# Moving the output stores and token loads of a two-layer MoE kernel's second part from SyncE's queue to GpSimd's

## The chip, the cores and the metric

The kernel runs on one core of a Trainium2 chip. The metric is the device time of one execution in microseconds. Before the change the median of three runs is 1465.66 us (1464.34 to 1467.58).

## The reference

The reference computes attention with pooled keys and values, then two feed-forward layers, all in float32:

```python
k_p = k.reshape(B, H, Sp, pool, D).mean(axis=3)        # B = H = 8, S = 576, D = 64, pool = 8
v_p = v.reshape(B, H, Sp, pool, D).mean(axis=3)
attn = softmax(q @ k_p^T / sqrt(D))                    # (its sum gets 1e-9 added)
x = (attn @ v_p) as 4608 tokens x 512
h = maximum(maximum(x @ w1, x @ w2), x @ w3)           # d_ff 768
x = h @ moe_w_out                                      # 4608 x 512
h = maximum(x @ w_in, 0.0)                             # d_ff 2048
out = (h * h) @ w_out                                  # 4608 x 512
```

## The kernel before

Each operand of the large products is split into a high and a low part (`split`: ScalarE rounds the high part, VectorE or GpSimd subtracts it), and a product is three matmuls: high by high, high by low, low by high.

**Part 1**, to 753 us, is attention and the first layer, in 12 blocks of 384 tokens. Its results, the tokens of the second layer, are written to `y_dram`. Beside it, the second layer's weights are combined, split and written to `wi_dram` and `wo_dram`. The change touches nothing of part 1.

**Part 2** is the second layer, in nine blocks (`NB2`, here called blocks 0 to 8) of 512 tokens. Each matrix product of 2 x 2 sub-matrices is done with seven products of sums and differences in place of eight. A block has four groups of hidden units (`gr` 0 to 3, here groups 0 to 3), each with two steps:

- `moe2_in` runs seven products of tokens `y` and weights `wi2s` (L688, 12 matmuls each), into PSUM tiles `ps` of which there are three. VectorE adds each to what came before (L659, tiles `c` and `a`); ScalarE and VectorE square.
- `moe2_out` runs four products in groups 0 and 1 and ten in groups 2 and 3 (L812, 12 matmuls each) into the PSUM tiles accA, accB, accD, accE and accF. Each has an operand `g`, made by `operand` and `split` (L134 on ScalarE, L135 on VectorE), and a weight tile `wo2s` of 512 KB, used once. In groups 2 and 3 the order is B, A, E, A, D, D, B, F, E, F.

The weights `wi2s` stay in SBUF. The tiles `wo2s` are fetched anew for every product (`fetch_out`, L616), 28 in a block, into a pool of five buffers (`wo_p`). So the fetch for a product can start when the fifth product before it has ended.

Block `j + 1`'s tokens are loaded by `load_y` (L631) while block `j` is in group 2. There are four tiles `yr`, each in two parts, and a part that spans two first-layer blocks takes two transfers, so a block has 8 or 12. The tiles share their places with operands of groups 0 to 2 and can be loaded when these have been read. `mix_y` and `split_y` then make seven operands `y` of the four tiles, on VectorE and ScalarE, beside group 3; the first of these is the difference `t<-yr` (L662). `evacuate` sums the accumulators and calls `store_out` (L768) four times in group 3: `o`, `o`, `qB`, `qA`, 256 KB each.

All these transfers are issued by SyncE, which issues in order, and waits for a transfer's buffer or data before it goes on to the next. The order on each engine is set by the tile scheduler, which simulates the program while it is built and places each instruction when its inputs and its engine are ready in that simulation. Moving a transfer to another queue so moves instructions on the other engines as well.

Of the kernel before, what the change touches and what calls it, by code (L numbers as in the profile page):

```python
# [20 lines left out]
P = 128  # L21
# [15 lines left out]
NB2 = NT // T2  # L37
# [57 lines left out]
def attention_moe_kernel(ctx: ExitStack, tc: tile.TileContext, q, k, v, vn, w1, w2, w3, wo1, wi2, wo2, out):  # L95
    nc = tc.nc
# [11 lines left out]
    for sign, base in ((1, POOL * MID), (-1, POOL - 1 - POOL * MID)):  # L108
        nc.gpsimd.affine_select(
            out=sums, in_=sums, compare_op=ALU.is_ge, fill=0.0, base=base,  # L110
# [8 lines left out]
    y_dram = [dram.tile([KD, P, T1], F32, name=f"y_dram{j}") for j in range(NB1)]  # L119
# [462 lines left out]
    for f in range(0, KF2, 2):  # L582
        rows = []
# [3 lines left out]
        rows = []  # L587
# [31 lines left out]
    def shared_place(i, shape, name):  # L619
        return y_p.tile(shape, F32, tag=f"r{i}", name=name)  # L620

    def load_y(j):

        for n, (r, h) in enumerate(((0, 0), (0, 1), (1, 0), (1, 1))):
            yr = shared_place(n, [P, 2, HT], "yr")
            for i in range(2):
                t = 0
                while t < HT:
                    b, o = divmod(j * T2 + h * HT + t, T1)
                    n = min(HT - t, T1 - o)  # L630
                    nc.sync.dma_start(out=yr[:, i, t : t + n], in_=y_dram[b][2 * r + i, :, o : o + n])  # L631
                    t += n
            yr_t[j, r, h] = yr

# [28 lines left out]

    ORDER = (1, 6, 7, 5, 2, 4, 3)
    early = [functools.partial(load_y, 0), functools.partial(mix_y, 0)]
    early.append(functools.partial(fetch_in, 0, w2_p))
    early += [functools.partial(split_y, 0, m) for m in ORDER]
# [97 lines left out]

    def store_out(j, half, d, o):
        rows = out[j * T2 + half * HT : j * T2 + (half + 1) * HT, d * 256 : (d + 1) * 256]
        nc.sync.dma_start(out=rows.rearrange("(i p) d -> p i d", p=P), in_=o.rearrange("p (i d) -> p i d", i=2))  # L768

    def evacuate(j, b, n):  # L770

        acc = made[b][0]
        if b in "AB" and n == HALF:
            q = made["q" + b] = c_p.tile([P, T2], F32, tag="q" + b, name="q" + b)
            nc.scalar.activation(q, acc, AF.Copy)
        if n < FULL[b]:
            return
        q = made["qA"]
        if b == "A":
            o = c_p.tile([P, T2], F32, tag="c3", name="o")  # L780
            nc.scalar.activation(o, acc, AF.Copy)
            store_out(j, 0, 0, o)
        elif b == "D":
            add(q, acc, q)
        elif b == "B":
            o = c_p.tile([P, T2], F32, tag="c2", name="o")
            add(o, acc, q)
            store_out(j, 1, 0, o)
        elif b == "E":
            add(q, acc, q)  # L790
            add(made["qB"], made["qB"], q)
            store_out(j, 1, 1, made["qB"])
        else:
            add(q, acc, q)
            store_out(j, 0, 1, q)
        del made[b]
# [32 lines left out]
    for j in range(NB2):  # L829
        for gr in range(NG):  # L830
            more = j + 1 < NB2
            c = moe2_in(j, gr)

            if gr == NG - 1 and more:
                mix_y(j + 1)
                for y in ORDER[:4]:
                    split_y(j + 1, y)
            for n, (m, h) in enumerate(OUT[gr >= NG // 2]):
                if gr == NG - 1 and more and n in (4, 6, 8):
                    split_y(j + 1, ORDER[2 + n // 2])  # L840
                moe2_out(j, gr, m, h, c)
            if gr == NG - 2 and more:
                load_y(j + 1)
            nxt = j * NG + gr + 1
            if nxt < NB2 * NG:
                fetch_group(nxt % NG)
# [41 lines left out]
```

## Time and profile before

| | |
|---|---|
| runs, median of 3 | 1465.66 us (1464.34 to 1467.58) |
| the profiled execution: its time | 1463.68 us |
| the profiled execution: its span, first to last instruction | 1462.0 us |
| part 2, from 753.3 us on | 708.7 us |
| TensorE / VectorE / ScalarE / GpSimd busy over the span | 98% / 67% / 52% / 12% |
| mean granted clock of TensorE, share of full speed | 0.993 |
| transfers by SyncE's queue | 261.61 MB |

A profile covers one execution. Engines are PE (TensorE's matmuls), PEld (its weight loads), DVE (VectorE), ACT (ScalarE), POOL (GpSimd) and SP (SyncE); "SPq" is SyncE's queue, whose time is not counted as busy. A row names the line of the kernel, the operation and its tiles as out<-in. In the timeline a row is a run of instructions of one group: its start and length in microseconds, how many, and in brackets the idle time before it and what ended it. Matmuls are pipelined, so their shown lengths overlap.

### The profile page before, as it was taken

To read this page: it belongs to the slowest core of one execution; us is meant where nothing else is said; L and a number is where in the kernel's file an instruction comes from. 1 tells how busy PE (TensorE), PEld (TensorE's weight loads), DVE (VectorE), ACT (ScalarE), POOL (GpSimd) and SP (SyncE) were. 2 spreads that over 40 slices of the span, in tenths; PEclk is the share of its full clock that TensorE was granted. 3 is DMA by queue.
4 is the path that set the end of the run, shared out by engine and by line. 5 is a ranking of instruction groups with operands and counts; after the bars stand their busy time and mean duration, and the time that the engine had idled before them with its cause. 6 is when DMAs were issued, how large, how long until landed. Compare 5 with 4: busy or idle time off the path is not lost.

```text
span 1462.0 us, 27667 instructions
## 1 busy us (share of the span) xinstructions
PE 1426.7 (98%) x10410; PEld 1401.6 (96%) x10410; DVE 983.3 (67%) x1778; ACT 762.5 (52%) x1983; POOL 177.5 (12%) x229
## 2 busy tenths in 40 slices
PE   6889999999999999999999999999999999999998
PEld 4879999999999999999999999999999999999998
DVE  5896476766765856756336768686766768686775
ACT  7795366664666656654323545363534445454443
POOL 3441022311312212221000000000000000000000
PEclk9999999999999999999999999999999999999999
DMA  7654145543455544432549857666567665665746
GB/s 226 188 164 140 62 145 181 173 137 130 145 170 187 151 145 144 127 123 86 187 162 356 280 176 240 220 208 217 214 231 230 229 212 213 205 238 179 277 139 229
DMA packets 125029, 272.81 MB, mean 187 GB/s; under 512 B 13504, under 2 KB 69568, under 8 KB 124896
## 3 DMA queue, kind: packets, MB, share of 16 engines
q1 hardware_dynamic: 117984, 261.61, 53.4%
q10 hardware_dynamic: 6912, 9.44, 1.8%
q8 instruction: 82, 1.34, 0.4%
q14 instruction: 51, 0.42, 0.1%
HBM read 213.91 MB, written 48.23 MB: 179 GB/s over the span
## 4 chain that ended last, share of the span: by engine, by line
PE 89%; DMA 6%; ACT 3%; DVE 2%; issue 1%; SPq 0%; POOL 0%; DVEq 0%; ACTq 0%; POOLq 0%
PE ps L528 29%; PE ps L688 23%; PE ps L547 10%; PE accB L812 6%; PE accA L812 6%; PE accF L812 3%; DMA wo2s<-wo_dram 3%; PE accE L812 3%; PE accD L812 2%; PE sc L362 2%; ACT ss L367 1%; PE tr L395 1%; PE av L425 1%; PE av L424 1%; DMA kq<-in_k_dram 1%
## 5 line engine op out<-in xcount | busy, mean ns | idle before, releaser
L528 PE MATMUL ps<-x,w 128*128 128x384 f32 x2592 | 493.8, 341 | 5.3 <-ACT w L134 2.7
L528 PEld LDWEIGHTS ps<-x,w 128*128 128x128 f32 x2592 | 449.6, 189 | 8.5 <-ACT w L134 3.0
L688 PE MATMUL ps<-y,wi2s 128*128 128x256 f32 x3024 | 371.5, 277 | 0.5 <-DVE c L659 0.2
L688 PEld LDWEIGHTS ps<-y,wi2s 128*128 128x128 f32 x3024 | 356.6, 188 | 1.5 <-DVE a L659 0.7
L547 PE MATMUL ps<-h,wo 128*128 128x384 f32 x864 | 162.2, 339 | 0.1
L547 PEld LDWEIGHTS ps<-h,wo 128*128 128x128 f32 x864 | 149.2, 188 | 0.7 <-POOL wo L135 0.4
L701 ACT ACTIVATE c<-c 128x512 f32<-128x512 f32 x90 | 56.3, 627 | 169.7 <-DVE c L659 169.1
L659 DVE TENSOR_TENSOR c<-ps,c 128x512 f32<-128x512 f32 x144 | 98.2, 687 | 67.3 <-PE ps L688 64.4
L536 DVE TENSOR_TENSOR hm<-ps,hm 128x384 f32<-128x384 f32 x144 | 79.6, 552 | 76.6 <-PE ps L528 73.6
L134 ACT ACTIVATE g<-c 128x512 fp32r<-128x512 f32 x144 | 90.3, 627 | 56.9 <-DVE c L698 23.3
L812 PE MATMUL accA<-wo2s,g 128*128 128x256 f32 x864 | 115.7, 277 | 0.0
L812 PE MATMUL accB<-wo2s,g 128*128 128x256 f32 x864 | 111.1, 277 | 4.5 <-DMA wo2s<-wo_dram 3.5
L812 PEld LDWEIGHTS accB<-wo2s,g 128*128 128x128 f32 x864 | 104.0, 188 | 5.7 <-issue 1.9
L135 DVE TENSOR_TENSOR g<-c,g 128x512 fp32r<-128x512 f32 x144 | 97.8, 685 | 16.5 <-ACT g L134 16.4
L812 PEld LDWEIGHTS accA<-wo2s,g 128*128 128x128 f32 x864 | 107.1, 188 | 0.0
L367 ACT ACTIVATE ss<-sc,st 128x72 f32<-128x72 f32 (+1 forms) x320 | 98.0, 321 | 15.0 <-DVE st L364 12.0
L373 POOL TENSOR_TENSOR ss<-ss,st 128x432 f32<-128x432 f32 (+1 forms) x64 | 53.7, 839 | 238.8 <-DVE st L372 96.4
L400 DVE TENSOR_TENSOR pt<-tr,pt 72x192 fp32r<-72x192 f32 (+1 forms) x112 | 48.8, 448 | 46.5 <-ACT pt L399 44.9
L427 ACT ACTIVATE xf<-av 64x192 f32<-64x192 f32 (+1 forms) x112 | 45.4, 405 | 58.8 <-PE av L425 47.5
L428 DVE TENSOR_TENSOR xf<-av,xf 64x192 f32<-64x192 f32 (+1 forms) x112 | 50.8, 453 | 36.7 <-ACT xf L427 34.8
L134 ACT ACTIVATE h<-hm 128x384 fp32r<-128x384 f32 x72 | 37.6, 522 | 57.1 <-DVE hm L536 56.4
L367 ACT ACTIVATION_READ_ACCUMULATOR ss<-sc,st 128x1 f32 (+1 forms) x320 | 66.3, 207 | 0.0
(107 smaller groups left out, 1936.5 us busy)
## 6 DMA issues: line engine op xcount, KB each, us to landing
wo2s<-wo_dram SPq DMA_DIRECT2D x252, 512.0 KB
wi2s<-wi_dram SPq DMA_DIRECT2D x24, 512.0 KB
wraw<-in_wo_dram SPq DMA_DIRECT2D x22, 512.0 KB
wraw<-in_w_dram SPq DMA_DIRECT2D x18, 512.0 KB
y_dram<-ys ACTq DMA_DIRECT2D x48, 192.0 KB
wraw<-in_wi_dram SPq DMA_DIRECT2D x16, 512.0 KB
wi_dram<-wraw SPq DMA_DIRECT2D x16, 512.0 KB
wo_dram<-wraw SPq DMA_DIRECT2D x64, 128.0 KB
```

Source lines behind the costliest of these rows:

```text
L134: nc.scalar.activation(hi, src, AF.Copy)
L135: engine.tensor_tensor(out=lo, in0=src, in1=as_f32(hi), op=ALU.subtract)
L367: nc.scalar.activation(ss[:, i, h], src[:, i, h], AF.Exp, bias=st[:, 0, i, h : h + 1], accum_out=st[:, 1, i, h : h + 1],)
L373: nc.gpsimd.tensor_tensor(out=ss, in0=ss, in1=st[:, 2].rearrange("p g (h o) -> p g h o", o=1).to_broadcast([m, g, 2, SP]), op=ALU.mult,)
L428: nc.vector.tensor_tensor(out=xf[r], in0=av[r], in1=xf[r], op=ALU.add)
L528: nc.tensor.matmul(ps, lhsT=w1_t[f, e][:, a, kk * P : (kk + 1) * P], rhs=x[kk][:, c], start=(n == 0), stop=(n == 3 * KD - 1),)
L536: nc.vector.tensor_tensor(out=hm, in0=ps, in1=hm, op=ALU.max)
L547: nc.tensor.matmul(ps, lhsT=wo1_t[kk][:, a, d * P : (d + 1) * P], rhs=hs[kk][:, c], start=(n == 0), stop=(n == 3 * KF1 - 1),)
L659: nc.vector.tensor_tensor(out=out, in0=in0, in1=in1, op=ALU.add)
L688: nc.tensor.matmul(bank[:, u * HT : (u + 1) * HT], lhsT=wi2_t[2 * gr + u][i][:, a, o + kk * P : o + (kk + 1) * P], rhs=y_t[j][m][:, c, kk] ...
L701: nc.scalar.activation(c, c, AF.Relu)
L812: nc.tensor.matmul(bank[:, i * 256 : (i + 1) * 256], lhsT=g[:, a, u * HT + i * P : u * HT + (i + 1) * P], rhs=w[:, u, c], start=(n == 0 an ...
```

## The change

The diff is whole:

```diff
     def load_y(j):
 
+        queue = nc.gpsimd if j else nc.sync
         for n, (r, h) in enumerate(((0, 0), (0, 1), (1, 0), (1, 1))):
             yr = shared_place(n, [P, 2, HT], "yr")
             for i in range(2):
@@
-                    nc.sync.dma_start(out=yr[:, i, t : t + n], in_=y_dram[b][2 * r + i, :, o : o + n])
+                    queue.dma_start(out=yr[:, i, t : t + n], in_=y_dram[b][2 * r + i, :, o : o + n])
@@
     def store_out(j, half, d, o):
         rows = out[j * T2 + half * HT : j * T2 + (half + 1) * HT, d * 256 : (d + 1) * 256]
-        nc.sync.dma_start(out=rows.rearrange("(i p) d -> p i d", p=P), in_=o.rearrange("p (i d) -> p i d", i=2))
+        queue = nc.gpsimd if j + 1 < NB2 else nc.sync
+        queue.dma_start(out=rows.rearrange("(i p) d -> p i d", p=P), in_=o.rearrange("p (i d) -> p i d", i=2))
```

The token loads of blocks 1 to 8 (84 transfers) and the stores of blocks 0 to 7 (32) are issued by GpSimd. Block 0's loads, in part 1, and the last block's stores stay with SyncE. Lines after L624 have one or two added to their numbers.

On SyncE, before, this stands where block 6's tokens are loaded in block 5 (`yr` are the token tiles, `wo2s` the weights, the numbers behind y_dram its blocks, counted from 128):

```order
L631 DMA yr<-y_dram_136 128x128
L631 DMA yr<-y_dram_137 128x128
L616 DMA wo2s<-wo_dram_0_0_116 128x1024
L631 DMA yr<-y_dram_136 128x256 x2
L616 DMA wo2s<-wo_dram_0_0_108 128x1024
```

On GpSimd, after, the same loads and the stores of the block stand like this, and SyncE has the weights alone:

```order
L632 DMA yr<-y_dram_136 128x128
L632 DMA yr<-y_dram_137 128x128
L632 DMA yr<-y_dram_136 128x256 x4
L770 DMA out_dram<-o 128x2x256 x2
L770 DMA out_dram<-qB 128x2x256
L770 DMA out_dram<-qA 128x2x256
```

The loads and stores have moved from between the weights to one queue of their own, the loads first.

On TensorE, before, in group 3 of block 5, from the last matmuls of the first accA product (the x4 of accA, which end it) to the second accB product:

```order
L812 MATMUL accA<-wo2s,g 128x256 x4
L812 MATMUL accE<-wo2s,g 128x256 x8
L812 MATMUL accA<-wo2s,g 128x256 x12
L812 MATMUL accD<-wo2s,g 128x256 x8
L688 MATMUL ps<-y_14434,wi2s_1_8638 128x256 x2
L812 MATMUL accD<-wo2s,g 128x256 x16
L812 MATMUL accB<-wo2s,g 128x256 x12
```

After, the same place, from the accA row whose first four matmuls end the first accA product (`ps<-y` belongs to the next block):

```order
L814 MATMUL accA<-wo2s,g 128x256 x12
L689 MATMUL ps<-y_14431,wi2s_2_8299 128x256
L689 MATMUL ps<-y_14434,wi2s_1_8297 128x256
L814 MATMUL accE<-wo2s,g 128x256 x4
L814 MATMUL accD<-wo2s,g 128x256 x8
L689 MATMUL ps<-y_14434,wi2s_1_8297 128x256 x5
L689 MATMUL ps<-y_14434,wi2s_1_8638 128x256 x3
L814 MATMUL accA<-wo2s,g 128x256 x4
L689 MATMUL ps<-y_14434,wi2s_1_8638 128x256 x3
L689 MATMUL ps<-y_14431,wi2s_2_8299 128x256
L814 MATMUL accB<-wo2s,g 128x256 x8
```

More of the next block's matmuls stand inside the group, and the second accB product, the seventh of the group, starts before the first accD product has ended. Between the end of the first accA product, which frees the seventh product's weight buffer, and the start of that product there were 46 matmuls and are 38.

On VectorE, before, in block 5, from the last operand of group 2 on (`t<-yr` is the first use of the next block's tokens, `c<-ps` the additions of group 3):

```order
L135 TENSOR_TENSOR g<-c_14013,g 128x512
L662 TENSOR_TENSOR t_14424<-yr 128x512
L659 TENSOR_TENSOR c_14316<-ps,c_14315 128x512
L135 TENSOR_TENSOR y_14427<-yr,y_14427 128x512
L662 TENSOR_TENSOR yr<-yr 128x512
L659 TENSOR_TENSOR yr<-yr 128x512
L659 TENSOR_TENSOR c_14317<-ps,c_14316 128x512
```

After:

```order
L135 TENSOR_TENSOR g<-c_14013,g 128x512
L660 TENSOR_TENSOR c_14316<-ps,c_14315 128x512
L660 TENSOR_TENSOR c_14317<-ps,c_14316 128x512
L660 TENSOR_TENSOR c_14318<-ps,c_14317 128x512
L660 TENSOR_TENSOR c_14315<-ps,c_14315 128x512
L663 TENSOR_TENSOR t_14424<-yr 128x512
L135 TENSOR_TENSOR y_14504<-yr,y_14504 128x512
```

The first use of the tokens has moved from before the first addition to behind the fourth. In blocks 1, 2, 4, 5 and 7, where the next block's tokens come in twelve transfers, it stands behind four or five additions (before, behind one or none); in blocks 3 and 6 behind one and in block 0 behind four, as it did.

## Rows read from the trace of the kernel before

**Rows 1.** The page: busy time of the engines, and the chain that ended last.
```profile
PE 1426.7 (98%) x10410; PEld 1401.6 (96%) x10410; DVE 983.3 (67%) x1778; ACT 762.5 (52%) x1983; POOL 177.5 (12%) x229
...
PE 89%; DMA 6%; ACT 3%; DVE 2%; issue 1%; SPq 0%; POOL 0%; DVEq 0%; ACTq 0%; POOLq 0%
```

**Rows 2.** Busy time by stretch: block 0, blocks 1 to 7, the rest.
```profile
core 0: us, PE busy (x) PEld busy (x) DVE busy (x) ACT busy (x) POOL busy (x), PEclk, DMA share, GB/s
753.30:862.00 108.70, 105.92 (x910) 104.57 (x910) 72.84 (x114) 46.08 (x79) 0.00 (x0) 1.00 0.81 294
862.00:1406.00 544.00, 540.69 (x4706) 538.50 (x4705) 396.96 (x631) 252.28 (x434) 0.00 (x0) 1.00 0.63 217
1406.00:1462.00 56.00, 50.23 (x437) 49.70 (x435) 35.16 (x56) 22.97 (x39) 0.00 (x0) 0.99 0.59 198
```

**Rows 3.** TensorE's waits from 862 to 1406 us: total, times, longest.
```profile
PE accB L812 <- DMA wo2s<-wo_dram: 1.9, 3, 0.9
PE accF L812 <- DMA wo2s<-wo_dram: 1.1, 3, 0.6
```

**Rows 4.** Timeline of PE: waits for weights in group 2 of blocks 0 and 4.
```profile
811.56 1.65 PE L812 MATMUL accF<-wo2s,g 128*128 128x256 f32 x12 [1.62 <-DMA wo2s<-wo_dram]
...
1119.44 1.65 PE L812 MATMUL accB<-wo2s,g 128*128 128x256 f32 x12 [0.93 <-DMA wo2s<-wo_dram]
```

**Rows 5.** The waits of SyncE's queue from 753 us on.
```profile
SPq L616 <- PE accA L812: 195.5, 59, 9.8
SPq L616 <- PE accB L812: 144.6, 57, 11.7
SPq L631 <- DVE g L135: 59.4, 14, 8.0
```

**Rows 6.** The chain in group 3 of block 5: start, length, what.
```profile
1216.94 0.92 PE accE L812 x8
1217.86 0.02 issue
1217.88 6.11 DMA wo2s<-wo_dram
...
1224.12 1.65 PE accF L812 x12
...
1228.44 1.36 PE accF L812 x12
```

**Rows 7.** Timeline of SyncE in the same place.
```profile
1217.88 0.32 SPq L616 DMA_DIRECT2D wo2s<-wo_dram  x1
...
1219.23 0.32 SPq L616 DMA_DIRECT2D wo2s<-wo_dram  x1
1219.87 0.39 SPq L768 DMA_DIRECT2D out_dram<-o  x1
```

**Rows 8.** Stretches of block 3: with token loads, then with full buffers.
```profile
1032.50:1047.00 14.50, 14.50 (x129) 14.50 (x128) 9.40 (x15) 5.22 (x9) 0.00 (x0) 1.00 0.90 317
1052.00:1059.40 7.40, 7.40 (x67) 7.40 (x67) 7.38 (x13) 7.05 (x14) 0.00 (x0) 1.00 0.00 1
```

**Rows 9.** Timeline of SyncE: first and last token loads in block 5.
```profile
1188.83 0.32 SPq L631 DMA_DIRECT2D yr<-y_dram  x1
...
1195.59 2.85 SPq L631 DMA_DIRECT2D yr<-y_dram  x4
```

**Rows 10.** Timeline of VectorE, then of PE, in block 5.
```profile
1202.51 0.69 DVE L662 TENSOR_TENSOR t<-yr 128x512 f32<-128x512 f32 x1 [4.24 <-DMA yr<-y_dram]
...
1208.65 0.68 DVE L659 TENSOR_TENSOR c<-ps,c 128x512 f32<-128x512 f32 x1
...
1203.69 8.80 PE L688 MATMUL ps<-y,wi2s 128*128 128x256 f32 x76
```

**Rows 11.** Groups of GpSimd's instructions: the longest mean.
```profile
L135 POOL TENSOR_TENSOR wo<-wbits,wo 128x512 fp32r<-128x512 f32 x6 | 8.6, 1447 | 8.0 <-ACT wo L134 6.3 <-DMA ssr<-ss 1.8
```

**Rows 12.** The chain from 753 us on: weights it waited for, in blocks 1, 3, 7 and 8.
```profile
905.73 5.24 DMA wo2s<-wo_dram
...
1064.63 7.57 DMA wo2s<-wo_dram
...
1372.60 6.14 DMA wo2s<-wo_dram
...
1445.77 4.19 DMA wo2s<-wo_dram
```

## The prediction

> **What bounds the kernel now.** I read the page's head first: TensorE is busy for 98% of the span, and the chain that ended last is 89% TensorE [rows 1]. The change touches only part 2 (the second layer, nine blocks, from 753.3 us), so that stretch comes next. In the 544 us of blocks 1 to 7 TensorE is busy for 540.69, at a granted clock of 1.00, and VectorE for 396.96, 73%; GpSimd does nothing [rows 2]. Moved transfers make no matmul shorter, so only idle time can be won or lost: 3.3 us there and 108.70 - 105.92 = 2.8 us in block 0. The last block keeps its queue and loads no tokens, so its 5.8 us stay.
>
> Then the waits. In blocks 1 to 7 TensorE waited six times for a weight tile of the second layer, 3.0 us in all [rows 3]; block 0 has one more, 1.62 [rows 4]. A matmul is shown 0.276 us long, while twelve take 1.36 us (0.1135 each, rows 6), so each gap hides another 0.16: 3.0 + 1.62 + 7 x 0.16 = 5.7 us. Nothing the change does to weights can win more than a little over that.
>
> Does the queue make these weights late? SyncE stood 195.5 + 144.6 us before a weight fetch because TensorE had not released one of the five buffers, and 59.4 us before a token load [rows 5]. One late weight, followed through: accE's product ends at 1217.86, the fetch into its buffer is issued at 1217.88 and lands 6.11 us later, when accF has already waited [rows 6]. The store of that stretch goes out at 1219.87, after it [rows 7]. The fetch was on time at the queue and slow in the engines: at 512 KB per 1.36 us the dense stretch asks for 385 GB/s; in block 3's stretch with token loads the engines gave 317 at a share of 0.90, and then stood at 0.00 while all five buffers were full [rows 8].
>
> **The change, part by part.** It takes 84 token loads (8 or 12 in each of eight blocks) and 32 stores off SyncE.
>
> *Issue time on SyncE*: 0.32 to 0.7 us each (rows 7, 9), some 50 us in all. Taken at 0: the queue waits over 340 us for buffers, and those waits only grow. Without that cover, a fetch behind a token load would go out one issue earlier, 0.3 to 0.7 us.
>
> *Bytes* stay as they are. Group 2's waits (1.62 in block 0, 0.93 in block 4, rows 4; 2.9 with what the gaps hide) fall among the token loads, which still come then. Between -2.9 (both gone) and +2.9 (doubled); taken -0.7, a quarter, since in block 4 the loads came in bursts.
>
> *TensorE's new order* is the term that decides. A weight has from the release of its buffer until its product for landing. Counted in the order of group 3 as matmuls between the two, for the sixth to the tenth product: before 45, 46, 53, 53, 59 (50, 50 in the middle in blocks 2 and 5); after 72, 49, 48, 52, 70 in blocks 1, 4, 7, then 64, 38, 54, 50, 40 in blocks 2, 5, and 37, 40, 44, 48, 60 in blocks 3, 6. In time, at 0.1135 each, the seventh weight had 5.2 us before and has 5.6, 4.3 or 4.5 after. What it needs: the late ones took 5.24 to 7.57 us, and 4.19 in the last block, with few others in flight [rows 12].
> Blocks 1, 4, 7 gain room for the sixth and tenth weight: their waits go. In blocks 2 and 5 the seventh (4.3 us) is late by 0.1 to 0.9; I take 0.8 with the tenth (4.5). In blocks 3 and 6 four weights in a row have 4.2, 4.5, 5.0 and 5.4 us against 5.24 to 6.14; the lateness of one is room for the next, so 0.9 once. After: 2 x 0.8 + 2 x 0.9 = 3.4. Before: rows 3 without block 4's 0.93, 2.1 in five waits, with 5 x 0.16 hidden 2.9. Cost +0.5, between -2.9 (no waits are left) and +4 (some 1.7 us late in each of blocks 2, 3, 5 and 6, less the 2.9 of before). In group 2 of blocks 2 and 5 the seventh has 44 in place of 49, 0.6 us less: +0.3 each, +0.6.
>
> *The token loads on GpSimd*. It has nothing else to do in part 2 [rows 2]; they queue behind each other and before the block's stores. The trace doesn't show what one costs there. The ends are SyncE's issue of the same transfer, 0.32 us [rows 9], and GpSimd's longest kind of instruction, 1.447 [rows 11]; I take 0.9, the middle, as the transfer is that of the one row and the engine that of the other. VectorE waits for them, in order, at t<-yr, and behind that stand the additions that empty PSUM. In block 5, t waited 4.24 us for them until 1202.51, and TensorE ran on without a gap [rows 10]. After, four additions stand ahead of t, the fourth of which ran at 1208.65, so t is wanted at some 1208. Twelve loads from 1188.83, and the 4.1 us from the last issue's end (1195.59 + 2.85) to t [rows 9, 10]: 1188.83 + 12 x 0.9 + 4.1 = 1203.7, early by 4. Break-even is (1208 - 1188.83 - 4.1) / 12 = 1.26 us a load; at 1.447 they are 2.3 us late in each of the five blocks with twelve loads, at most 11.5 us. At 0.32 nothing is won, since t stands where it stands. Taken 0.
> The Trainium skill (DMA: Bandwidth & Descriptors, Specifications) gives about 1 us to the first byte for GpSimd's path, 0.6 for the other; an estimate by it, 12 x 1 us, has t ready at 1204.9, so also 0. No run here shows it.
>
> *VectorE's later work*: the next block's subtractions and splits move behind the additions, into the time of group 3's operands. The 4.24 us it stood before t now hold the four additions (4 x 0.6). Taken 0; up to 0.4 a block, 3 us, stays in the range.
>
> Sum: -0.7 + 0.5 + 0.6 = +0.4. Against the profiled execution (1463.68 us, its span 1462.0) that is 1464.1; it lies 1.98 under the median of the three runs, 1465.66, so in medians 1466.1.
>
> **The rivals.** *Weight waits go*: if token loads and stores ahead of a weight are what slows it, most of 5.7 us come back; 4.5 gives 1461.2. For it: in block 4 six token loads stand in a row before the next weights, and the waits fall where either is near. Against it: the late weights went out at the release.
>
> *Slower, by late tokens*: above 1.26 us a load, t is late, the in-order VectorE leaves PSUM banks full, and TensorE stops. At 1.447 up to 11.5; half of it, as a free bank covers about a product of 1.36 us: 1465.66 + 5.8 = 1471.5. For it: VectorE already waits over 4 us here. Against it: the order puts t four or five additions later in just the blocks with twelve loads.
>
> *Slower, by the tighter order*: the scheduler takes the freed queue at its word, and the engines don't deliver: the bounds above, +4 and +0.6, with group 2's waits left: 1470.3.
>
> The Trainium skill has a rule against the change (DMA: Bandwidth & Descriptors, Issuing engines are not separate DMA queues): transfers of all issuers run on the same 16 engines, and another issuer saves issue time only. By it the time stays at 1465.7. The trace agrees in that the late fetch above was not late at the queue; the order of matmuls, which the rule leaves out, does change.
>
> **How the numbers follow.** Under 0.2% (2.9 us) can't be told from no change. Forecast, 1466.1, own range 1463 to 1469: 0.48 (0.40 within, 0.04 on either side). Weight waits go: 0.25 (0.23 beyond 2.9, 0.02 within). Late tokens 0.15, tighter order 0.12, both slower by over 2.9. Sums: faster 0.27, same 0.42, slower 0.31. The range for 8 in 10 runs from the first rival, less half a microsecond, to the second and half a microsecond: 1460.7 to 1472.
>
> **What would show it.** SyncE's waits in part 2 should be for TensorE's buffers, with no token load among them. TensorE's waits for weights should stay near 3 us in blocks 1 to 7, but leave blocks 1, 4, 7 and grow in 2, 3, 5, 6, at the second accB product (blocks 2, 5) and accF. VectorE's wait before t should be under 1 us; several us there, with TensorE waiting on an addition at L660, is the late-token rival. If the weights' waits fall under 1 us in all, the loads and stores in the old queue had slowed them, and my reading of the late fetch is wrong. If TensorE waits on L135's operands, VectorE's later work costs what I put at 0.

## The result, and the profile after

The changed kernel takes 1477.75 us (median of 6 runs, 1475.31 to 1478.77), the kernel before 1466.01 beside it (6 runs, 1464.34 to 1468.41). The ratio is 1.0083, 95% interval 1.0071 to 1.0095: slower by 12 us. No change was forecast, and the time lies outside the range.

The profiled execution took 1478.0 us, its span 1476.3. The page's head, and the chain that ended last:

```profile
PE 1433.0 (97%) x10410; PEld 1405.4 (95%) x10410; DVE 981.1 (66%) x1778; ACT 762.5 (52%) x1983; POOL 245.9 (17%) x345
...
PE 84%; DMA 5%; DVE 5%; ACT 4%; issue 1%; POOL 0%; DVEq 0%; POOLq 0%; ACTq 0%
```

VectorE's share of the chain has gone from 2% to 5% [rows 1]. The first sign: more of the path runs through it, though its busy time has not grown. Busy time by the stretches of [rows 2]:

```profile
753.30:862.00 108.70, 106.34 (x904) 104.83 (x903) 71.46 (x112) 45.32 (x78) 7.38 (x12) 1.00 0.81 297
862.00:1406.00 544.00, 532.89 (x4607) 528.03 (x4606) 389.29 (x623) 249.27 (x430) 60.75 (x104) 1.00 0.61 213
1406.00:1477.00 71.00, 63.74 (x546) 63.38 (x544) 41.59 (x66) 26.55 (x45) 0.00 (x0) 0.97 0.55 186
```

Read the counts of matmuls. In block 0's stretch there are 6 fewer than before, in blocks 1 to 7 another 99. At 0.1135 us each that is 0.7 and 11.2 us. The rest of the program has 109 more (12.4 us); the last instruction ends at 1476.3, so this part is 14.3 us longer and has lost 1.9 itself. The loss therefore lies in blocks 1 to 7, 1.6 us in each on the mean. TensorE's waits there, in the columns of [rows 3]:

```profile
PE accE L814 <- DMA wo2s<-wo_dram: 3.7, 4, 1.4
PE accB L814 <- DVE g L135: 2.1, 3, 0.7
PE ps L689 <- DVE y L135: 2.0, 2, 1.0
PE accB L814 <- DMA wo2s<-wo_dram: 1.3, 2, 0.9
PE accB L814 <- ACT g L134: 0.7, 1, 0.7
PE accF L814 <- DMA wo2s<-wo_dram: 0.4, 1, 0.4
```

Two kinds have come. Weights: 3.7 + 1.3 + 0.4 = 5.4 us against 3.0, most of it at accE. Operands and tokens that VectorE and ScalarE make: 4.8 us, where before had none. With two smaller kinds the waits come to 10.7 us in 16 (before 3.0 in 6), and the ten gaps more hide another 1.6: 9.3 of the 11.2 us. The rest shows in no wait.

One stretch shows both. The chain in block 4, from the late accE weight of group 2 to the first accB product of group 3 (start, length, what):

```profile
1122.25 7.45 DMA wo2s<-wo_dram
...
1129.83 1.65 PE accE L814 x12
...
1137.67 0.64 ACT y L134
...
1138.34 0.56 DVE y L135
...
1140.83 0.60 DVE t L663
1141.43 0.61 DVE g L135
...
1142.09 0.74 PE accB L814 x4
```

The weight went out at its buffer's release and took 7.45 us, with token loads in flight beside it. Then TensorE waits for `g`, in front of which VectorE has the tokens' `y` and `t` to make, among additions. VectorE's timeline in that place:

```profile
1132.27 0.69 DVE L660 TENSOR_TENSOR c<-ps,c 128x512 f32<-128x512 f32 x1 [5.21 <-PE ps L689]
1134.95 0.69 DVE L660 TENSOR_TENSOR c<-ps,c 128x512 f32<-128x512 f32 x1 [1.99 <-PE ps L689]
...
1137.67 0.69 DVE L660 TENSOR_TENSOR c<-ps,c 128x512 f32<-128x512 f32 x1 [0.67 <-PE ps L689]
...
1140.75 0.68 DVE L663 TENSOR_TENSOR t<-yr 128x512 f32<-128x512 f32 x1
1141.35 0.68 DVE L135 TENSOR_TENSOR g<-c,g 128x512 fp32r<-128x512 f32 x1
```

Up to the first addition it stands, as it did before. Between the four additions it stands another 1.99 + 0.67 + 0.67 us, since each waits for TensorE; the kernel before put `t` and the tokens' first splits there. From 1137.67 on it runs without a pause. Ahead of `g` it now has two pieces of the tokens' work; before there were nine, most of them between the additions. TensorE's own rows there, before and after, and VectorE's `g` before:

```profile
1126.35 8.80 PE L688 MATMUL ps<-y,wi2s 128*128 128x256 f32 x76
1134.99 1.07 PE L812 MATMUL accB<-wo2s,g 128*128 128x256 f32 x8
...
1138.00 0.62 PE L812 MATMUL accB<-wo2s,g 128*128 128x256 f32 x4
```
```profile
1133.60 6.76 PE L689 MATMUL ps<-y,wi2s 128*128 128x256 f32 x58
1140.20 1.07 PE L814 MATMUL accB<-wo2s,g 128*128 128x256 f32 x8
...
1142.09 0.74 PE L814 MATMUL accB<-wo2s,g 128*128 128x256 f32 x4 [0.70 <-DVE g L135]
```
```profile
1135.89 0.68 DVE L135 TENSOR_TENSOR g<-c,g 128x512 fp32r<-128x512 f32 x1
```

The accB product now stands 58 matmuls behind the last accF product in place of 76. Its last four matmuls, which need VectorE's `g`, began 11.65 us after the start of these rows before (1138.00 - 1126.35), and 8.49 after, wait included. Without the wait it would be 7.79: TensorE asks for `g` 3.9 us sooner. VectorE has `g` ready sooner too, 8.4 us after the start of the rows in place of 10.2, but only by 1.8 us. In blocks 2 and 5 TensorE waits for the tokens' own split `y`, which now stands behind the additions: 2.0 us in two waits.

GpSimd's issues, then the loads' median time to landing in blocks 1 to 7 (KB each, us):

```profile
L632 POOL DMA_DIRECT2D yr<-y_dram x84 | 45.1, 542 | 379.6 <-DVE g L135 355.8 <-ACT g L134 17.1 <-DMA yr<-y_dram 4.5
```
```profile
yr<-y_dram POOLq DMA_DIRECT2D x36, 128.0 KB, 5.8
yr<-y_dram POOLq DMA_DIRECT2D x40, 64.0 KB, 5.7
```

A load takes 0.54 us of GpSimd, less than the 0.9 assumed, and lands 5.7 or 5.8 us after issue, later than the 4.1 assumed.

### The profile page after: what moved, and what is told of

It is laid out like the page before. It is cut to its first block, busy times and chain, and to the rows that moved or that the text cites. A ratio compares the mean times of both kernels' runs of the same rounds, so it can differ in the third digit from the quotient of the medians.

```text
span 1476.3 us, 27716 instructions
## 1 busy us (share of the span) xinstructions
PE 1433.0 (97%) x10410; PEld 1405.4 (95%) x10410; DVE 981.1 (66%) x1778; ACT 762.5 (52%) x1983; POOL 245.9 (17%) x345
## 3 DMA queue, kind: packets, MB, share of 16 engines
q1 hardware_dynamic: 97184, 244.82, 49.5%
q0 software_dynamic: 5952, 16.78, 3.3%
## 4 chain that ended last, share of the span: by engine, by line
PE 84%; DMA 5%; DVE 5%; ACT 4%; issue 1%; POOL 0%; DVEq 0%; POOLq 0%; ACTq 0%
PE ps L528 28%; PE ps L689 21%; PE ps L547 10%; PE accA L814 6%; PE accB L814 6%; DMA wo2s<-wo_dram 3%; PE accE L814 3%; PE accF L814 3%; PE sc L362 2%; PE accD L814 2%; ACT ss L367 2%; DMA vr<-in_v_dram 1%; DVE g L135 1%; PE av L425 1%; PE tr L395 1%
## 5 line engine op out<-in xcount | busy, mean ns | idle before, releaser
L814 PE MATMUL accB<-wo2s,g 128*128 128x256 f32 x864 | 114.1, 279 | 8.1 <-DMA wo2s<-wo_dram 3.8
L135 DVE TENSOR_TENSOR g<-c,g 128x512 fp32r<-128x512 f32 x144 | 97.8, 684 | 16.8 <-ACT g L134 16.8
L632 POOL DMA_DIRECT2D yr<-y_dram x84 | 45.1, 542 | 379.6 <-DVE g L135 355.8
```

The lines of the kernel that those rows point to most:

```text
L135: engine.tensor_tensor(out=lo, in0=src, in1=as_f32(hi), op=ALU.subtract)
L814: nc.tensor.matmul(bank[:, i * 256 : (i + 1) * 256], lhsT=g[:, a, u * HT + i * P : u * HT + (i + 1) * P], rhs=w[:, u, c], start=(n == 0 an ...
```

## The experiments

Ratios are against runs of the kernel before on the same chip (its median there 1463.3 to 1463.9 us). Three theories: **O**, the new order of instructions costs the time; **S**, transfers on another queue run beside the weights and both come later; **G**, GpSimd's way of issuing is slow.

With only the stores moved, TensorE, VectorE and ScalarE keep the order of the kernel before, row for row. With only the loads moved, VectorE and ScalarE have that of the changed kernel, and TensorE all but 28 of its 10,410 places. So the loads alone bring the order.

**1. Stores alone**

```diff
-        queue = nc.gpsimd if j else nc.sync
+        queue = nc.sync
```

> Only the stores of blocks 0 to 7 are issued by GpSimd; the tokens stay on SyncE. The order of TensorE's, VectorE's and ScalarE's instructions is then that of the kernel before, to the row. Theory O (the new order of instructions costs the 12 us, not the queues): 1466 us, no change within 2. Theory S (the moved transfers run beside the weights instead of behind them and make weights late): stores are 16.8 MB as the tokens are, a store lies in the way of group 2's and 3's weights like a token load, so some 3 to 6 of the 12 us: 1469 to 1472. Theory G (GpSimd's own issue is slow): stores nothing waits for, 1466.

1463.64 us, ratio 0.9998 (0.9988 to 1.0007). Nothing, and S is wrong for stores. (Its profiled run, 1470.5, was the longest of 13, so its waits aren't read.)

**2. Token loads alone**

```diff
-        queue = nc.gpsimd if j + 1 < NB2 else nc.sync
+        queue = nc.sync
```

> Only the token loads are issued by GpSimd; the stores stay on SyncE. The order on VectorE and ScalarE is then that of the changed kernel, on TensorE nearly. Theory O: all of it, 1477 to 1478 us. Theory S: the tokens' share, 1472 to 1475, and the weights' waits of group 2 (accE) stay. Theory G: 1477.

1476.49 us, ratio 1.0083 (1.0067 to 1.0100): the whole loss is the loads'. O and G gave it; S's 1472 to 1475 is just under.

**3 and 4. Queues and order apart.** The program is built once with the other queues, and the order found there is imposed by edges that set the order of issue on an engine (TensorE, VectorE, ScalarE) and wait for nothing:

```diff
+                for names in order.values():
+                    for a, b in zip(names, names[1:]):
+                        if a in traced and b in traced:
+                            tc.add_manual_dep(traced[b], a, QUIET, reason="order")
```

New queues, old order:

> Stores and token loads on GpSimd as in the changed kernel, but TensorE, VectorE and ScalarE are held to the order of the kernel before, instruction by instruction. Theory O: 1463 to 1467 us, VectorE stands some 4 to 7 us at the subtraction that needs the next tokens, as before, and TensorE's waits for operands made by VectorE go. Theory S: the weights of group 2 stay late beside the token loads, five or six waits of 0.3 to 1.6 us, so 1472 to 1476. Theory G: tokens are wanted some 5 us earlier than in the changed kernel; twelve loads took 16.7 us there from the first issue to the last landing, against 13.7 before, so VectorE is 3 us later in each block and TensorE stops: 1475 or more.

1474.68 us, ratio 1.0074 (1.0061 to 1.0086), 10.9 us. O is wrong as the only cause. S's range holds it, and G's bound is 0.3 us off. The timeline of GpSimd, of VectorE, then of TensorE, in block 5; the waits of the last two in blocks 1 to 7; and, last, VectorE's in the kernel before:

```profile
1203.16 1.07 POOL L633 DMA_DIRECT2D yr<-y_dram  x2 [0.69 <-DVE g L136]
...
1210.25 0.69 DVE L664 TENSOR_TENSOR t<-yr 128x512 f32<-128x512 f32 x1 [5.60 <-DMA yr<-y_dram]
1210.86 0.68 DVE L661 TENSOR_TENSOR c<-ps,c 128x512 f32<-128x512 f32 x1
...
1214.12 6.06 PE L690 MATMUL ps<-y,wi2s 128*128 128x256 f32 x47 [0.60 <-DVE c L661]
```
```profile
PE ps L690 <- DVE c L661: 7.0, 10, 1.3
...
DVE t L664 <- DMA yr<-y_dram: 29.5, 7, 6.4
```
```profile
DVE t L662 <- DMA yr<-y_dram: 16.3, 7, 4.5
```

`t` waits 29.5 us in seven blocks for tokens, 13.2 more than before; the addition behind it empties a PSUM bank late, and TensorE stops. In block 5 it begins 6.0 us after the last load's issue has ended (1203.16 + 1.07); before it was 4.1. This is the prediction's late-token rival, in an order that the scheduler did not choose.

Old queues, new order:

> Stores and token loads on SyncE as in the kernel before, but TensorE, VectorE and ScalarE are held to the order of the changed kernel, instruction by instruction. Theory O: 1475 to 1479 us, with TensorE's waits for VectorE's operands in blocks 1, 4, 7 and for the next block's tokens split late in blocks 2, 5 as in the changed kernel. Theory S: about 1466 plus what the operands cost (some 5 us in the changed kernel's waits), at most 1471. Theory G: 1466.

1473.37 us, ratio 1.0060 (1.0047 to 1.0073), 8.8 us: above S's 1471 and a little under O's range. The operands' waits are those of the changed kernel, on the old queue:

```profile
PE accB L815 <- DVE g L136: 2.1, 3, 0.7
PE ps L690 <- DVE y L136: 2.0, 2, 1.0
...
PE accE L815 <- DMA wo2s<-wo_dram: 1.6, 4, 0.4
```

So either alone costs 9 to 11 us, and both together 12: the new order takes away the wait for late tokens and brings another loss of nearly the same size.

**5. Which engine's order**

> Old queues. TensorE alone is held to the order of the changed kernel; VectorE and ScalarE keep that of the kernel before. With all three held to the new order the old queues took 8.8 us more (1.0060). Theory V (VectorE's later subtractions and splits cost it: TensorE's waits of 2.1 + 2.0 + 1.7 us for operands and tokens): 1464 to 1466 us, those waits go. Theory P (the tighter place of accB's and accE's products, against the release of their weight buffers, costs it): 1469 to 1473, with waits for weights of 4 us or more in blocks 1 to 7.

1479.32 us, ratio 1.0115 (1.0096 to 1.0135), more than with all three. Both theories miss. TensorE's waits in blocks 1 to 7, and one of them in block 4:

```profile
PE accB L815 <- DVE g L136: 4.3, 3, 1.5
PE accB L815 <- ACT g L135: 4.0, 5, 1.1
```
```profile
1144.21 1.22 PE L815 MATMUL accB<-wo2s,g 128*128 128x256 f32 x4 [1.44 <-DVE g L136]
```

With VectorE's old order the same accB product waits longer for its operand (1.44 us in place of 0.70). It is TensorE's order that asks too soon; VectorE's new order makes up part of it. Waits for weights add 6.0 us (2.7 at accE, 2.2 at accB, 1.1 at accF), and a stretch of 3.4 us at the lower clock is part of this kernel's size (last section). The profiled run was the longest of five (1483.24). VectorE's new order with TensorE's old one wasn't tried, so what VectorE's later work costs by itself isn't measured.

**6. A second queue that isn't GpSimd's.** As 3, with the stores on SyncE and

```diff
+        queue = nc.scalar if j else nc.sync
```

> The token loads of blocks 1 to 8 are issued by ScalarE, a queue of the same kind as SyncE's and apart from it; the stores stay on SyncE; TensorE, VectorE and ScalarE hold the order of the kernel before. On GpSimd with that order VectorE stood 2.2 to 6.4 us at the subtraction that needs the tokens (before 0.9 to 4.5), and the kernel took 10.9 us more. Theory G (what is late is GpSimd's way of issuing: its loads land 5.5 to 6.5 us after issue): VectorE's wait there is 1 to 4.5 us as before, 1463 to 1466 us. Theory S (a second queue shares the engines with the weights, whoever issues it): VectorE waits 2 to 6 us, 1470 to 1475. ScalarE's own time for an issue, 8 or 12 a block of some 0.4 us, may add up to 3 us where ScalarE waits for a release.

1491.79 us (1481.70 to 1495.83), ratio 1.0192 (1.0165 to 1.0220). The tokens are late here as well, though GpSimd issues none: `t` waits 16.3 + 11.1 us in seven blocks, before 16.3. That speaks against G, but doesn't settle it: the size is beyond S's, and ScalarE, which issues the loads between its own instructions, adds to it. The profiled run was the shortest of the six by 8 us. First the waits of TensorE and VectorE; in the last rows ScalarE stands for transfers of weights, which none of its instructions reads, behind the loads that it issues:

```profile
PE ps L690 <- DVE c L661: 12.6, 11, 3.7
```
```profile
DVE t L664 <- DMA yr<-y_dram: 16.3, 5, 3.7
DVE t L664 <- DMA wo2s<-wo_dram: 11.1, 2, 5.7
```
```profile
ACT g L135 <- DMA wo2s<-wo_dram: 9.6, 4, 3.0
...
ACT c L724 <- DMA wo2s<-wo_dram: 8.7, 3, 3.7
```

**7 and 8. Half as many loads, twice the size**

```diff
-                    queue.dma_start(out=yr[:, i, t : t + n], in_=y_dram[b][2 * r + i, :, o : o + n])
+                    rows = y_dram[b][2 * r : 2 * r + 2, :, o : o + n]
+                    queue.dma_start(out=yr[:, :, t : t + n], in_=rows.rearrange("k p t -> p k t"))
```

> Token loads and stores on GpSimd as in the changed kernel and the order of the kernel before on TensorE, VectorE and ScalarE, but each token load takes both halves of its tile: 4 or 6 loads a block in place of 8 or 12, the same bytes. With 8 or 12 it took 10.9 us more than before (1.0074). Theory N (the number of loads makes them late, 0.54 us of GpSimd each, one behind the other): six loads fewer are 3 us, so tokens come 1 to 3 us earlier, VectorE's wait falls to 1 to 4 us, and the kernel takes 1464 to 1468. Theory S (bytes beside the weights): the last load lands as late, 1472 to 1475.

1470.98 us, ratio 1.0059 (1.0041 to 1.0076), between the two ranges: at most a few of the 10.9 us are the number of loads (0.0074 less 0.0059 of 1466 is some 2, but the intervals overlap). Most of the loss stays, in another form: TensorE's waits for additions fell from 7.0 to 1.8 us in blocks 1 to 7, those for weights rose from 2.2 to 4.8.

> The kernel before with 4 or 6 token loads a block in place of 8 or 12, on SyncE, and the order that the scheduler then finds, which is neither that of before nor that of the changed kernel. Theory R (any other order than that of before costs some 5 to 10 us): 1469 to 1473 us. Theory O2 (only the late mixing of tokens and the tight weights of the changed kernel's order cost): 1461 to 1465.

1463.17 us, ratio 0.9997 (0.9986 to 1.0007), with another matmul than before, by tiles and shape, in 496 of TensorE's 10,410 places (1225 in the changed kernel). So not every other order costs. Nor does every wait for tokens: VectorE stood 24.6 us at `t`, and TensorE 0.2 us for an addition.

**9 to 11. Half the weights' bytes.** In groups 2 and 3 the second half of each weight tile is left out and the first is used twice, so the sums are not the reference's:

```diff
+        k = 1 if gr >= NG // 2 else 2
-        nc.sync.dma_start(out=as_f32(w), in_=wo2_dram[m, gr % 2, h])
+        nc.sync.dma_start(out=as_f32(w[:, :k]), in_=wo2_dram[m, gr % 2, h][:, :k])
-                        rhs=w[:, u, c], start=(n == 0 and k == 0),
+                        rhs=w[:, 0 if gr >= NG // 2 else u, c], start=(n == 0 and k == 0),
```

> In groups 2 and 3 of every block only the first half of each second-layer weight tile is fetched (256 KB in place of 512) and multiplied twice; same matmuls, the queues and the order of the kernel before. It is the base for the next two kernels. TensorE's waits for weights in blocks 1 to 7 (3.0 us in six waits) and block 0's 1.6 should go, with what the gaps hide some 4 to 6 us: 1457 to 1460 us.

1454.07 us, ratio 0.9937 (0.9922 to 0.9953): more than expected, 9.3 us. No wait for weights is left in blocks 1 to 7.

> The same with half the weights' bytes in groups 2 and 3 and the order of the kernel before, but tokens and stores on GpSimd. With whole weights these queues took 10.9 us more than the kernel before. Theory S (the tokens are late because weights that went out ahead of them share the engines): with half the bytes they are not; VectorE's wait at t falls by 2 us or more a block, and the kernel is within 3 us of the one with half weights on the old queues. Theory G (what makes them late is the issue of loads, by GpSimd or one by one): the loads land 5 us or more after issue still, TensorE waits 5 us or more for VectorE's additions, and the kernel is 8 to 11 us above the one on the old queues.

1455.13 us, 1.1 above the one on the old queues, within the noise (10.9 with whole weights): S's forecast, and G is wrong. The loads, from the same issuer and in the same number, now land in

```profile
yr<-y_dram POOLq DMA_DIRECT2D x36, 128.0 KB, 4.1
yr<-y_dram POOLq DMA_DIRECT2D x40, 64.0 KB, 3.6
```

against 5.9 and 5.7 with whole weights in experiment 3. `t` still waits longer than on the old queues (12.9 us, 5.5 there), but no longer than TensorE can bear: it stands for 0.01 us in 538 (862 to 1400 us):

```profile
862.00:1400.00 538.00, 537.99 (x4716) 537.80 (x4715) 398.84 (x632) 253.49 (x435) 60.69 (x104) 1.00 0.46 152
```

> The changed kernel, its queues and its order, with half the weights' bytes in groups 2 and 3. Theory W (the new order costs because weights are wanted sooner after the release of their buffers): all waits for weights go and it stands within 2 us of the one with half weights on the old queues and in the old order. Theory V (it costs because VectorE's and ScalarE's operands and the next tokens' splits come late): those waits, 2.1 + 2.0 + 1.4 us and some 1.2 hidden in the gaps, stay, and it stands 5 to 8 us above.

1461.03 us, 7.0 above the old queues in the old order, 5.9 above the new queues in the old order. V forecast this (operands and tokens come late), and W, which has only the weights wanted sooner, is wrong. No weight is waited for, and the operands still are:

```profile
PE accB L817 <- DVE g L137: 2.1, 3, 0.7
PE ps L692 <- DVE y L137: 2.0, 2, 1.0
```

**12 to 15. A faster kernel by smaller weights?** Two tiles of 256 KB in ten buffers (`bufs=10`), and in the product

```diff
-        for a, c in PARTS:
-            for u in range(2):
+        for u in range(2):
+            for a, c in PARTS:
```

> A try at a faster kernel: the queues of the kernel before, each weight tile of the second layer as two of 256 KB in ten buffers of half the size, and a product takes its first half's six matmuls before its second half's. So a half's buffer is free 0.7 us sooner. If the weights' waits (5.7 us with what the gaps hide) come from too short a time between release and use: 1459 to 1462 us. If twice as many issues on SyncE hold the tokens back, or smaller transfers are slower: 1465 to 1470.

1467.02 us, ratio 1.0022 (1.0012 to 1.0031). TensorE's waits in blocks 1 to 7 (to 1400 us):

```profile
PE ps L694 <- DVE c L665: 4.2, 6, 1.3
PE accF L819 <- DMA wo2s<-wo_dram: 1.1, 4, 0.4
```

The weights' waits nearly went, and VectorE waited 30.0 us at `t` (before 16.3): the tokens came late on the one old queue too, in an order that isn't that of before.

> Weight tiles in two halves as in the last try, all on SyncE, and 4 or 6 token loads a block in place of 8 or 12. In weights_in_halves TensorE's waits for weights fell to 1.1 us, but VectorE stood 3.5 to 5.0 us at t in every block and TensorE 4.2 us for VectorE's additions. If the tokens were late by the number of issues between the weights' (20 weights and 12 loads in a stretch), this gives 1459 to 1463 us; if by the weights' bytes in front of and beside them, 1465 to 1468 as before this edit.

1477.78 us, ratio 1.0089 (1.0069 to 1.0109). Neither: the scheduler found another order, in which weights were waited for again (accB 8.2 us in seven waits).

> The same, and the stores of blocks 0 to 7 on GpSimd, which cost nothing and won nothing alone (0.9998); the order of instructions is the same as without. 1459 to 1463 us if SyncE's issues count, within 1 us of the one without if they don't.

1477.10 us, ratio 1.0094 (1.0076 to 1.0111), 0.7 us under the one without, within 1 us: the stores' issues don't count.

> The same as the first, with TensorE, VectorE and ScalarE held to the order of the kernel before (within a product the first half's six matmuls come first). If the order that the scheduler found for the halves is what leaves TensorE waiting for VectorE's additions, this is 3 us or more faster than the first, 1457 to 1460; if not, within 1 us of it.

1470.22 us, ratio 1.0042 (1.0026 to 1.0058): 7 us better by the order alone, with no wait for a weight in blocks 1 to 7, and still slower than the kernel before: TensorE waits 6.1 us at accB for VectorE's `g`. With one half's six matmuls first, a product asks for the low part of `g` after four matmuls in place of eight, which may be why. No kernel tried beats it with its whole work.

## Why the prediction was wrong

*Issue time on SyncE, 0*: right. SyncE now waits 228.1 and 205.5 us for accA's and accB's buffers [rows 5], and stores alone or half as many loads change nothing (0.9998, 0.9997).

*Bytes, -0.7*: wrong in sign. In blocks 1 to 7 TensorE's waits for group 2's weights rose from 0.93 us, at accB in block 4 [rows 4], to 5.1, of which accE has 3.7. The new order on the old queues has 2.0 there, the new queues in the old order 0.3, where TensorE stops for additions first; so it is the two together. The error was to see only what stands ahead of a weight in its queue. Moved to another queue, the same loads run beside it.

*Token loads on GpSimd, 0*: right at its place, by two errors that offset each other. `t` waits 0.9 us once, in seven blocks; but the issue is 0.54 us, not 0.9, and the landing later. With the order of before the lateness costs 10.9 us, of which all but 1.1 go with half the weights' bytes. The rival "late tokens" was rejected because "the order puts t four or five additions later". It does; the price then came from the order itself.

*TensorE's new order, +0.5 and +0.6*: the step that failed. It counted only one resource, the weight between release and use, and put the operand `g` of the same product at nothing without a reason. `g` is wanted 3.9 us sooner, and VectorE makes it only 1.8 us sooner. The order alone, on the old queues, cost 8.8 us, not 1.1. For weights the forecast was too high in group 3: 3.4 us, and in blocks 1 to 7 one wait of 0.32 is left there, in block 6. In group 2 I counted too little: counted in the same way, the ninth product (accE) has 54 matmuls for its weight in place of 60 in blocks 1, 3, 4, 6 and 7, 0.7 us less, and TensorE's four waits at accE stand in blocks 1, 3, 4 and 7.

*VectorE's later work, "Taken 0; up to 0.4 a block, 3 us"*: failed with it. I set the 4.24 us that VectorE stood before `t` [rows 10] against four additions of 0.6 and took them for room. The additions can't move up into that time, since they wait for TensorE; VectorE now stands there as long for PSUM (5.21 us in block 4), and the tokens' `y` of blocks 2 and 5 come late. The sign named for this, TensorE waiting on L135's operands, came. But the later work isn't shown to be the cause of the waits for `g`: with VectorE's old order under TensorE's new one they are longer (experiment 5).

With the weights' part taken out, the new order costs 6 to 7 us. The 5 to 6 more with whole weights go with the weights' bytes (12 with the second queue, 8.8 without); TensorE's waits for weights show 2.4 of it (5.4 less 3.0), and where the rest lies stays open. The weights' bytes cost more than their waits in the kernel before too: half of them won 9.3 us, where the prediction saw 5.7 to win.

By a rule of the Trainium skill (DMA: Bandwidth & Descriptors, Issuing engines are not separate DMA queues) another issuer saves only issue time. Here, with the order held, it cost 10.9 us. Another section of that page (SWDGE vs HWDGE vs iDMA) says that each DMA engine takes turns between its queues; the landing times of 5.7 and 3.6 us with whole and half weights agree, though no run shows the turns.

In the profiled run a further 1.9 us lie in the last stretch: one weight landed later than before in the same place (TensorE waits 2.52 us, before 1.64), and the matmuls behind it ran at a lower clock (below), 0.9 us each. Whether the later landing belongs to the change stays open; nothing there was tried apart. Open too is why the scheduler puts the tokens' use so late when GpSimd issues them.

## What to carry to other kernels

A queue that several kinds of transfers share in order is also a priority. Before you give the urgent small ones a queue of their own, ask what will then run beside them; here the landing of the 64 KB loads went from 3.6 to 5.7 us when the weights beside them had twice the bytes. And where a scheduler sets the order, the change to forecast is the new order: follow each moved product to all of its inputs, operands as well as weights, and count idle time as room only for work whose inputs are there.

## What the runs showed of the hardware

A long wait can be paid twice. In the last block of the changed kernel TensorE waited 2.52 us, and its granted clock then was 0.50, the lower of its two levels, for 3.4 us, in which eight matmuls took 2.05 us; before, behind a wait of 1.64 us in the same place, they took 1.17 and the clock stayed at 1.00. The row of after:

```profile
1463.33 2.05 PE L814 MATMUL accB<-wo2s,g 128*128 128x256 f32 x8 [2.52 <-DMA wo2s<-wo_dram]
```

Where the tokens were loaded by ScalarE the same came with TensorE's waits of 3.66 and 2.36 us, and that is part of that kernel's size. In experiment 3 waits of up to 1.3 us in blocks 1 to 7 did not bring it. In experiment 5 a wait of 1.06 us and, eight matmuls and one more later, one of 1.44 did: the clock was 0.50 for 3.4 us from 1144.06 on, and the four matmuls of the row shown there took 1.22 us, 0.74 in the changed kernel's row.

GpSimd issued a load of 64 or 128 KB in 0.54 us and a store of 256 KB in 0.71 to 0.73. The same 16.8 MB of tokens and stores took 20,800 packets on SyncE's queue (117,984 less 97,184) and 5,952 on GpSimd's. ScalarE, when it issued the loads, stood 9.6 + 8.7 us in blocks 1 to 7 before its own arithmetic, for transfers that this arithmetic doesn't read; the kernel before shows no such wait at these instructions.
